# Six of eight f pairs by seven products, and four of their low parts on VectorE

## The chip, the cores and the metric

The kernel runs on one core of one Trainium2 chip. The metric is device time in microseconds, the median of several executions. Before the change it is 857.11 us over three runs (855.28 to 857.62).

## The reference

Strided and local attention over 8 batches, 8 heads, 576 positions and head size 64 gives `x` of 4608 tokens by 512. A feed-forward layer follows, and all of it is float32:

```python
h = x @ w_in            # 4608 x 512 by 512 x 2048
g = h * np.cos(h)
return (g @ w_out)      # 4608 x 2048 by 2048 x 512
```

## The kernel before, in words

The first stage (some 480 us) does the attention and `h = x @ w_in`, and writes `h` to DRAM as `h_all`. The second stage computes `g = h cos(h)` and `g @ w_out`. The change touches the second stage and, by one more set of weight sums, the end of the first.

The second stage walks over 18 blocks of 256 tokens (`s`); in each block it walks over 8 pairs of f tiles (`f`, 256 rows of `w_out` each). Every float32 factor is split into a high part (`g_hi`, a cast on ScalarE, line 183) and a low part (`g_lo`, the value minus its high part, line 184, on VectorE or GpSimd), and each product takes three matmuls: high by high, high by low, low by high (line 709).

A pair is multiplied in one of two ways. A plain pair takes 12 matmuls of 512 columns. A pair "by seven products" uses a Strassen-Winograd scheme on 2 by 2 blocks: 21 matmuls of 256 columns. For that, GpSimd first makes four sums of blocks of `g` (lines 674, 675 and 678, a chain of three instructions), and the split covers 896 columns instead of 512. `SEVEN` lists these pairs; in blocks 2 to 16 all of it holds, in block 1 the first three of it, and blocks 0 and 17 are plain throughout.

`gate(s, f)` (line 642) prepares a pair in four steps: load `h_in`; round on ScalarE and reduce the angle on VectorE (lines 654, 655); the sine on ScalarE, the product `g` on VectorE (line 664 for a plain pair, 673 for one by seven) and the sums on GpSimd; the split. `LEADS` says how many pairs ahead of the multiplication each step is issued (first tuple plain, second by seven). GpSimd's instructions for the gates are held in the order of issue by `by_gpsimd`. `BY_VECTOR` lists plain pairs whose low part is on VectorE. There the product lies in PSUM (tile `wave`); otherwise it lies in SBUF (`r`, or `g` for a pair by seven). Pools: `gp` holds 3 pairs of `g_hi`, `g_lo`; `rp` 3 tiles `r`; `sg` 3 tiles `wave`.

Five PSUM tiles (`q0` to `q4`) take the sums of a block in turn: lower and upper half of the output, and two (more, most) for terms of the seven products. At the end of a block VectorE adds them up (lines 747, 749, 752, then 761 twice), and the next block writes into the tiles that this frees: its upper half into the old "more" as soon as line 747 has read it, its "more" into the old "most" after line 752.

The weights' block sums are made and stored to DRAM in the first stage, loaded again (`t_all`) and split in the second; the last of them go through two buffers `t`.

Of the kernel before, what the change touches and what calls it, by code (L numbers as in the profile page):

```python
# [26 lines left out]
P = 128  # L27
# [52 lines left out]

TB = 2 * P
NTB = NTOK // TB
SEVEN = (4, 5, 6, 1, 2)
ROWS = (0, 3, 7)


LEADS = ((6, 4, 3, 2), (7, 4.5, 3.5, 2))
AHEAD = tuple(PER_BATCH - n for n in (20, 17, 13, 10, 7, 3))

BY_VECTOR = (0, 3, 7)  # L90


SUMMED = (14, 28, 36)
# [9 lines left out]
def attention_cos_ffn(ctx, tc, qkl, vl, qkvs, w_in, w_out, eye, eye16, mask_l0, mask_l, mask_s, out):  # L103
    nc = tc.nc
# [18 lines left out]
    w_all = dram.tile([NFC, P, DM], F32, name="w_all")  # L123
    t_all = dram.tile([len(SEVEN), P, 2 * DM], F32, name="t_all")

# [8 lines left out]
    def order(later, first, reason):  # L134
        tc.add_manual_dep(
            later.ins, first.ins.name,
            mybir.DependencyInfo(mybir.DependencyClass.NoSync, mybir.DependencyReason.DATA), reason=reason,
        )
# [12 lines left out]
    def with_product(begun):  # L151
        if turn is not None:
            order(begun, turn, "with this product")

    def weight_tile(f):
        pool, n = (by_rows, len(ROWS)) if f in ROWS else (wp, NF - len(ROWS))
        return pool.tile([P, 2, 2, 2 * P], F32R, name="w", bufs=2 * n)
# [24 lines left out]
    def split(x, hi, lo, cast=nc.scalar.copy, rest=nc.gpsimd):  # L182
        with_product(cast(out=hi, in_=x))  # L183
        return rest.tensor_tensor(out=lo, in0=x, in1=hi.bitcast(F32), op=ALU.subtract)  # L184
# [401 lines left out]
    def output_weights(room, n, rest=nc.gpsimd):  # L586
        both = room()
        t = weight_tile(n // 2).rearrange("p l m n -> p l (m n)")
        nc.sync.dma_start(out=both, in_=w_all[n])
        yield  # L590
        split(both, t[:, 0], t[:, 1], rest=rest)
        wo.append((t[:, 0], t[:, 1]))
        yield

    def whole_tile(cv):
        return cv.tile([P, 512, 2], I32, name="raw", bufs=3).bitcast(F32).rearrange("p n w -> p (n w)")

    def output_sums(cv, n):

        f = SEVEN[n]  # L600
        both = whole_tile(cv).rearrange("p (f n) -> p f n", f=2)
# [12 lines left out]
    def split_sums(room, n):  # L614
# [6 lines left out]
        split(t[:, :3], most[:, 0], most[:, 1])  # L621
        sums[SEVEN[n]] = [(most[:, 0, n], most[:, 1, n]) for n in range(3)]
        yield
# [3 lines left out]
        split(t[:, 3], *last)  # L627
        sums[SEVEN[n]].append(last)
        yield
# [3 lines left out]
    def seven(s, f):  # L633
        return 0 < s < NTB - 1 and f in SEVEN[:len(SUMMED) if s == 1 else len(SEVEN)]

    of_gates = []

    def by_gpsimd(begun):
        if of_gates:
            order(begun, of_gates[-1], "pair by pair")  # L640
        of_gates.append(begun)

    def gate(s, f):

        h = hp.tile([P, 2 * TB], F32, name="h_in")
        nc.sync.dma_start(
            out=h.rearrange("p (f t) -> p f t", f=2),
            in_=h_all[2 * f:2 * f + 2, :, s * TB:(s + 1) * TB].rearrange("f p t -> p f t"),
        )
        yield  # L650
        r = rp.tile([P, 2 * TB], F32, name="r")
        wave = sg.tile([P, 2 * TB], F32, name="wave")
        k = wave.bitcast(I32)
        with_product(nc.scalar.activation(out=k, in_=h, func=AF.Copy, scale=1.0 / (2.0 * math.pi), bias=0.25))  # L654
        nc.vector.scalar_tensor_tensor(out=r, in0=k, scalar=-2.0 * math.pi, in1=h, op0=ALU.mult, op1=ALU.add)  # L655
        yield
        sin = nc.scalar.activation(out=wave, in_=r, func=AF.Sin, bias=quarter)  # L657
        with_product(sin)
        if s == 0 and f == 0:
            order(sin, exps[-1], "one change of tables")  # L660
        pool = nc.gpsimd
        if not seven(s, f):
            low, pool = (wave, nc.vector) if f in BY_VECTOR else (r, nc.gpsimd)
            nc.vector.tensor_tensor(out=low, in0=wave, in1=h, op=ALU.mult)
            yield
            g_hi, g_lo = (gp.tile([P, 7 * P], F32R, name=name) for name in ("g_hi", "g_lo"))
            lo = split(low, g_hi[:, :4 * P], g_lo[:, :4 * P], rest=pool)
            if pool is nc.gpsimd:
                by_gpsimd(lo)
            gates[s, f] = g_hi, g_lo  # L670
            yield
        g = gs.tile([P, 8, P], F32, name="g")
        nc.vector.tensor_tensor(out=g[:, :4].rearrange("p n t -> p (n t)"), in0=wave, in1=h, op=ALU.mult)
        by_gpsimd(pool.tensor_tensor(out=g[:, 4], in0=g[:, 0], in1=g[:, 2], op=ALU.add))
        by_gpsimd(pool.tensor_tensor(  # L675
            out=g[:, 5:7], in0=g[:, 0:5:4], in1=g[:, 1:2].broadcast_to([P, 2, P]), op=ALU.subtract
        ))
        by_gpsimd(pool.tensor_tensor(out=g[:, 7], in0=g[:, 3], in1=g[:, 6], op=ALU.subtract))  # L678
        yield
        g_hi, g_lo = (gp.tile([P, 7 * P], F32R, name=name) for name in ("g_hi", "g_lo"))  # L680
        by_gpsimd(split(g[:, 1:].rearrange("p n t -> p (n t)"), g_hi, g_lo))
        gates[s, f] = g_hi, g_lo
        yield

    tiles = [(s, f) for s in range(NTB) for f in range(NF)]
    work = [gate(*tile) for tile in tiles]

    def ahead(at):
        for i, tile in enumerate(tiles):
            if i - at in LEADS[seven(*tile)]:  # L690
                next(work[i])
# [90 lines left out]
    with ExitStack() as phase:  # L782
# [18 lines left out]
        m, n, o = ((pools[name], name) for name in "mno")  # L801
# [62 lines left out]
        def in_steps(work, *slots):  # L864
            work = iter(work)
            for slot in slots:
                steps.setdefault(slot, []).append(partial(next, work, None))
# [10 lines left out]
        for n in range(NFC - LATE):  # L878
            at = (B - 1) * PER_BATCH + STEP * (n // 2) + 12 + 3 * (n % 2)
            in_steps(output_weights(lambda: whole_tile(cv)[:, :DM], n), at - 6, at)  # L880
        for n, f in enumerate(SEVEN):
            at = 2 * PER_BATCH + 17 * (2 * f + 2)
# [12 lines left out]
        for slot in range(max(*plan, *steps) + 1):  # L895
# [9 lines left out]
            if b == B - 1:  # L905
                if at == 0:
                    attention.close()
                    sg = ctx.enter_context(tc.tile_pool(
                        name="sg", bufs=3, space=bass.MemoryType.PSUM, side="right", reuse_waits="tile"
# [10 lines left out]

    op = ctx.enter_context(tc.tile_pool(name="op", bufs=2, reuse_waits="tile"))
    tp = ctx.enter_context(tc.tile_pool(name="tp", bufs=1, reuse_waits="tile"))
    gs = ctx.enter_context(tc.tile_pool(name="gs", bufs=3, reuse_waits="tile"))
    pools = {"q": ctx.enter_context(
        tc.tile_pool(name="ps_q", bufs=1, space=bass.MemoryType.PSUM, reuse_waits="tile")
    )}
# [2 lines left out]
    for n in range(NFC - LATE, NFC):  # L929
        rest = nc.vector if n % 2 else nc.gpsimd  # L930
# [115 lines left out]
```

## Time and profile before

| | |
|---|---|
| median of three runs | 857.11 us |
| profiled execution | 857.26 us, of which the span is 855.5 us |
| TensorE busy | 845.1 us, 99% of the span |
| VectorE, ScalarE, GpSimd busy | 567.4, 528.4, 539.7 us |
| mean granted TensorE clock | 0.998 of full speed |

The chain of waits is the row of work that ended last, followed back from the end; in the second stage it is all TensorE. The question for such a kernel is how long a block takes on TensorE, and how far the other engines are from being late for it.

### The profile page before, as it was taken

What the parts mean: (1) busy time and instruction counts of PE and PEld (TensorE: products, weight loads), DVE (VectorE), ACT (ScalarE), POOL (GpSimd) and SP (SyncE); (2) the same over time, 40 slices, a digit from 0 to 9 for tenths busy, and PEclk for the clock granted to TensorE, in tenths of its full rate; (3) what the DMA queues carried; (4) which work ended last, traced back from release to release, by engine and by line L of the source; (5) the groups of instructions that cost most, each with busy time, mean ns of one, the idle gap of its engine ahead of it and who ended that gap; (6) DMA issues with size and microseconds to landing.
All of it is one profiled execution on the core that took longest, in us unless ns stands there. A gap on an engine that the chain in (4) does not pass through costs nothing.

```text
span 855.5 us, 23160 instructions
## 1 busy us (share of the span) xinstructions
PE 845.1 (99%) x9147; PEld 785.3 (92%) x9147; DVE 567.4 (66%) x1087; ACT 528.4 (62%) x1031; POOL 539.7 (63%) x543
## 2 busy tenths in 40 slices
PE   9999999999999999999999999999999999999998
PEld 5799999999998999999999889999999999999996
DVE  5888755768658567676333667777777677767671
ACT  3766545545445354454456887777777777777772
POOL 2578984416207134162166478999899989898951
PEclk9999999999999999999999999999999999999999
DMA  9698444566666667665456844444444444444330
GB/s 333 189 297 296 145 163 165 178 214 207 224 222 208 230 222 226 227 213 210 155 195 222 280 135 129 131 124 125 129 131 124 132 128 124 134 126 136 120 127 26
DMA packets 91901, 151.82 MB, mean 177 GB/s; under 512 B 8464, under 2 KB 53008, under 8 KB 91792
## 3 DMA queue, kind: packets, MB, share of 16 engines
q1 hardware_dynamic: 91072, 150.11, 53.8%
q8 instruction: 72, 1.18, 0.6%
q14 instruction: 37, 0.30, 0.1%
q10 hardware_dynamic: 720, 0.23, 0.1%
HBM read 96.30 MB, written 54.00 MB: 176 GB/s over the span
## 4 chain that ended last, share of the span: by engine, by line
PE 90%; POOL 3%; ACT 2%; DVE 2%; DMA 1%; issue 1%; DVEq 0%; ACTq 0%; POOLq 0%
PE q L709 44%; PE m L532 19%; PE n L532 9%; PE o L532 5%; PE m L503 4%; PE acc L335 2%; PE acc L400 2%; PE acc L318 2%; POOL x_lo L184 2%; PE acc L387 1%; PE acc L811 1%; PE acc L370 1%; DMA h_all<-h 1%; DMA w_all<-sums 1%; PE m L370 0%
## 5 line engine op out<-in xcount | busy, mean ns | idle before, releaser
L709 PE MATMUL q<-w,g_hi 128*128 128x512 f32 (+1 forms) x1000 | 199.9, 338 | 0.0
L709 PEld LDWEIGHTS q<-w,g_hi 128*128 128x128 f32 x1000 | 159.7, 188 | 22.1
L184 POOL TENSOR_TENSOR g_lo<-g,g_hi 128x896 fp32r<-128x896 f32 x78 | 165.1, 2132 | 6.3 <-ACT g_hi L183 6.0
L709 PE MATMUL q<-w,g_lo 128*128 128x512 f32 (+1 forms) x500 | 111.4, 337 | 0.0
L532 PE MATMUL m<-x_hi,v 128*128 128x288 f32 x448 | 109.4, 299 | 0.8 <-ACT m L540 0.8
L532 PE MATMUL m<-x_hi,w 128*128 128x288 f32 x448 | 108.5, 298 | 0.4 <-DVE h L550 0.4
L655 DVE SCALAR_TENSOR_TENSOR r<-wave,h_in 128x512 f32<-128x512 int32 x144 | 96.1, 685 | 15.2 <-ACT wave L654 13.8
L657 ACT ACTIVATE wave<-r,quarter 128x512 f32<-128x512 f32 x144 | 98.6, 688 | 5.9 <-DVE r L655 5.9
L183 ACT CAST g_hi<-g 128x896 fp32r<-128x896 f32 x78 | 73.4, 941 | 39.6 <-POOL g L678 27.7
L709 PEld LDWEIGHTS q<-w,g_lo 128*128 128x128 f32 x500 | 82.7, 188 | 10.9
L654 ACT ACTIVATE wave<-h_in 128x512 int32<-128x512 f32 x144 | 83.6, 591 | 7.6 <-DVE g_lo L184 7.4
L709 PE MATMUL q<-v,g_hi 128*128 128x256 f32 x624 | 85.4, 279 | 0.0
L532 PEld LDWEIGHTS m<-x_hi,v 128*128 128x128 f32 x448 | 78.1, 188 | 2.1 <-ACT m L540 1.3
L532 PEld LDWEIGHTS m<-x_hi,w 128*128 128x128 f32 x448 | 78.0, 188 | 1.4 <-DVE h L550 0.7
L709 PEld LDWEIGHTS q<-v,g_hi 128*128 128x128 f32 x624 | 78.3, 188 | 0.0
L288 POOL TENSOR_TENSOR pn_s<-e_sb,z 128x324 f32<-128x324 f32 x28 | 20.9, 748 | 90.2 <-DVE z L286 84.0
L184 DVE TENSOR_TENSOR g_lo<-wave,g_hi 128x512 fp32r<-128x512 f32 x54 | 37.2, 689 | 53.2 <-PE q L709 36.0
L540 ACT COPY m<-m 128x288 f32<-128x288 f32 x112 | 44.5, 397 | 43.7 <-PE m L532 37.0
L288 POOL TENSOR_TENSOR e_sb<-e_sb,z 128x384 f32<-128x384 f32 x24 | 20.3, 844 | 77.6 <-DVE z L286 77.2
L532 PE MATMUL m<-x_lo,v 128*128 128x288 f32 x224 | 66.1, 295 | 0.0
L532 PE MATMUL m<-x_lo,w 128*128 128x288 f32 x224 | 65.9, 294 | 0.0
L675 POOL TENSOR_TENSOR g<-g 128x256 f32<-128x256 f32 x78 | 57.7, 740 | 6.1
(137 smaller groups left out, 2051.8 us busy)
## 6 DMA issues: line engine op xcount, KB each, us to landing
h_all<-h SPq DMA_DIRECT2D x128, 288.0 KB, 2.9
h_in<-h_all SPq DMA_DIRECT2D x144, 256.0 KB, 2.8
qk<-in_qkvs SPq DMA_DIRECT2D x28, 324.0 KB, 4.4
out<-o SPq DMA_DIRECT2D x35, 256.0 KB, 3.0
qk<-in_qkl SPq DMA_DIRECT2D x21, 416.0 KB, 4.4
raw<-in_w_in SPq DMA_DIRECT2D x16, 512.0 KB, 5.3
raw<-in_w_out SPq DMA_DIRECT2D x16, 512.0 KB, 4.8
v<-in_vl SPq DMA_DIRECT2D x24, 224.0 KB, 4.0
```

What stands on the lines that cost most here:

```text
L183: with_product(cast(out=hi, in_=x))
L184: return rest.tensor_tensor(out=lo, in0=x, in1=hi.bitcast(F32), op=ALU.subtract)
L288: nc.gpsimd.tensor_tensor(out=pn, in0=e, in1=z[:, :n].unsqueeze(2).broadcast_to([P, n, w]), op=ALU.mult)
L318: self.scored = self.pe(nc.tensor.matmul(s_ps[quarter_of(c), t * KW:(t + 1) * KW], q_t[half(j), p, QB * t:QB * (t + 1)], k_t[half(j), p, Q ...
L503: in_turn(nc.tensor.matmul(self.banks[i, j], a[:, c * P:(c + 1) * P], y[:, c], start=k == 0 and m == 0, stop=k == 1 and m == len(ops) - 1, ...
L532: in_turn(nc.tensor.matmul(bank, a[:, c * P:(c + 1) * P], y[:, c], start=first and i == 0, stop=i == len(ops) - 1, skip_group_check=True,))
L540: nc.scalar.copy(out=t, in_=self.bank[name[0]])
L654: with_product(nc.scalar.activation(out=k, in_=h, func=AF.Copy, scale=1.0 / (2.0 * math.pi), bias=0.25))
L655: nc.vector.scalar_tensor_tensor(out=r, in0=k, scalar=-2.0 * math.pi, in1=h, op0=ALU.mult, op1=ALU.add)
L657: sin = nc.scalar.activation(out=wave, in_=r, func=AF.Sin, bias=quarter)
L675: by_gpsimd(pool.tensor_tensor(out=g[:, 5:7], in0=g[:, 0:5:4], in1=g[:, 1:2].broadcast_to([P, 2, P]), op=ALU.subtract))
L709: in_turn(nc.tensor.matmul(at, a, w, start=first, stop=True, skip_group_check=True))
```

## The change

Pair 3 joins the pairs by seven products, in blocks 2 to 16. The gates by seven are begun a pair earlier (loads 8 pairs ahead, rounding 5.5, sine and sums 4.5; the split stays at 2), and `gs`, which holds `g`, has a fourth buffer. The low parts are dealt out anew: of pairs 1, 3, 4 and 6 on VectorE, of 0, 2, 5 and 7 on GpSimd, whichever way the pair is multiplied. Before, VectorE had those of the plain pairs 0, 3 and 7. Output weights of pair 3 are no longer kept in the pool `by_rows`, and a sixth set of weight sums is made, stored, loaded and split.

```diff
-SEVEN = (4, 5, 6, 1, 2)
-ROWS = (0, 3, 7)
+SEVEN = (4, 5, 6, 1, 2, 3)
+ROWS = (0, 7)

-LEADS = ((6, 4, 3, 2), (7, 4.5, 3.5, 2))
+LEADS = ((6, 4, 3, 2), (8, 5.5, 4.5, 2))

-BY_VECTOR = (0, 3, 7)
+BY_VECTOR = (1, 3, 4, 6)
...
         pool = nc.gpsimd
+        rest = nc.vector if f in BY_VECTOR else pool
         if not seven(s, f):
-            low, pool = (wave, nc.vector) if f in BY_VECTOR else (r, nc.gpsimd)
+            low = wave if f in BY_VECTOR else r
             nc.vector.tensor_tensor(out=low, in0=wave, in1=h, op=ALU.mult)
             yield
             g_hi, g_lo = (gp.tile([P, 7 * P], F32R, name=name) for name in ("g_hi", "g_lo"))
-            lo = split(low, g_hi[:, :4 * P], g_lo[:, :4 * P], rest=pool)
-            if pool is nc.gpsimd:
+            lo = split(low, g_hi[:, :4 * P], g_lo[:, :4 * P], rest=rest)
+            if rest is pool:
                 by_gpsimd(lo)
...
         g_hi, g_lo = (gp.tile([P, 7 * P], F32R, name=name) for name in ("g_hi", "g_lo"))
-        by_gpsimd(split(g[:, 1:].rearrange("p n t -> p (n t)"), g_hi, g_lo))
+        lo = split(g[:, 1:].rearrange("p n t -> p (n t)"), g_hi, g_lo, rest=rest)
+        if rest is pool:
+            by_gpsimd(lo)
...
-    gs = ctx.enter_context(tc.tile_pool(name="gs", bufs=3, reuse_waits="tile"))
+    gs = ctx.enter_context(tc.tile_pool(name="gs", bufs=4, reuse_waits="tile"))
```

Lines from 662 on move down by one to three: 664 becomes 665; 673, 674, 675, 678 become 674, 675, 676, 679; 747, 749, 752, 761 become 750, 752, 755, 764.

VectorE at the end of a steady block, before the change. `t` and `o` are the adding up of the block that ends, `q` its PSUM tiles, `wave` 10637 belongs to the plain pair 3 of the next block.

```order
L664 TENSOR_TENSOR wave_10637<-wave_10637,h_in_10561 128x512
L747 TENSOR_TENSOR t_10629<-q1_10430,t_10629 128x256
L749 TENSOR_TENSOR t_10629<-q2_10441,t_10629 128x512
L752 TENSOR_TENSOR t_10629<-q2_10441,t_10629 128x256
L673 TENSOR_TENSOR g_10683<-wave_10651,h_in_10563 128x512
L761 TENSOR_TENSOR o_10660<-q3_10400,t_10629 128x512
L761 TENSOR_TENSOR o_10663<-q4_10405,t_10629 128x512
L655 SCALAR_TENSOR_TENSOR r_10688<-wave_10689,h_in_10600 128x512
L184 TENSOR_TENSOR g_lo_10697<-wave_10637,g_hi_10696 128x512
```

The same place after the change; `g_lo` 10767 is the low part of pair 1 of the next block, 10829 that of pair 3.

```order
L674 TENSOR_TENSOR g_10779<-wave_10753,h_in_10654 128x512
L184 TENSOR_TENSOR g_lo_10767<-g_10671,g_hi_10766 128x896
L750 TENSOR_TENSOR t_10763<-q1_10551,t_10763 128x256
L752 TENSOR_TENSOR t_10763<-q2_10562,t_10763 128x512
L674 TENSOR_TENSOR g_10815<-wave_10785,h_in_10693 128x512
L755 TENSOR_TENSOR t_10763<-q2_10562,t_10763 128x256
L655 SCALAR_TENSOR_TENSOR r_10820<-wave_10821,h_in_10730 128x512
L764 TENSOR_TENSOR o_10794<-q3_10519,t_10763 128x512
L764 TENSOR_TENSOR o_10797<-q4_10524,t_10763 128x512
L184 TENSOR_TENSOR g_lo_10829<-g_10747,g_hi_10828 128x896
```

A low part of 896 columns stands ahead of the first addition, and another right behind the last; before, a low part of 512 columns out of PSUM stood one instruction behind the last.

VectorE in the second half of a block, before. `wave` 10775 and 10799 belong to pair 7 and the next pair 0, `g` 10852 to pair 1 of the next block.

```order
L664 TENSOR_TENSOR wave_10775<-wave_10775,h_in_10700 128x512
L655 SCALAR_TENSOR_TENSOR r_10816<-wave_10817,h_in_10741 128x512
L664 TENSOR_TENSOR wave_10799<-wave_10799,h_in_10739 128x512
L184 TENSOR_TENSOR g_lo_10828<-wave_10775,g_hi_10827 128x512
L673 TENSOR_TENSOR g_10852<-wave_10817,h_in_10741 128x512
```

And after; `g_lo` 10645 is the low part of pair 6, `g` 10671 the product of pair 1 of the next block.

```order
L655 SCALAR_TENSOR_TENSOR r_10633<-wave_10634,h_in_10549 128x512
L665 TENSOR_TENSOR r_10613<-wave_10614,h_in_10547 128x512
L655 SCALAR_TENSOR_TENSOR r_10650<-wave_10651,h_in_10584 128x512
L184 TENSOR_TENSOR g_lo_10645<-g_10568,g_hi_10644 128x896
L674 TENSOR_TENSOR g_10671<-wave_10634,h_in_10549 128x512
```

The product that GpSimd's next chain of sums starts from now stands behind a low part that reads `g` and `g_hi`, both in SBUF.

GpSimd in a steady block before: two chains of sums and their two low parts.

```order
L674 TENSOR_TENSOR g_10308<-g_10308 128x128
L675 TENSOR_TENSOR g_10308<-g_10308 128x256
L678 TENSOR_TENSOR g_10308<-g_10308 128x128
L674 TENSOR_TENSOR g_10345<-g_10345 128x128
L675 TENSOR_TENSOR g_10345<-g_10345 128x256
L678 TENSOR_TENSOR g_10345<-g_10345 128x128
L184 TENSOR_TENSOR g_lo_10361<-g_10308,g_hi_10360 128x896
L184 TENSOR_TENSOR g_lo_10395<-g_10345,g_hi_10394 128x896
```

And after: the low part of plain pair 0 (from `r`), the sums of pairs 3 and 4, and the low part of pair 2.

```order
L184 TENSOR_TENSOR g_lo_10442<-r_10365,g_hi_10441 128x512
L675 TENSOR_TENSOR g_10462<-g_10462 128x128
L676 TENSOR_TENSOR g_10462<-g_10462 128x256
L679 TENSOR_TENSOR g_10462<-g_10462 128x128
L675 TENSOR_TENSOR g_10494<-g_10494 128x128
L676 TENSOR_TENSOR g_10494<-g_10494 128x256
L679 TENSOR_TENSOR g_10494<-g_10494 128x128
L184 TENSOR_TENSOR g_lo_10516<-g_10425,g_hi_10515 128x896
```

There are six chains of sums in a block now, and two low parts of 896 columns and two of 512 between them, where there were five and five.

## Rows read from the trace of the kernel before

**Rows 1.** The page's first part: busy time of each engine.

```profile
span 855.5 us, 23160 instructions
...
PE 845.1 (99%) x9147; PEld 785.3 (92%) x9147; DVE 567.4 (66%) x1087; ACT 528.4 (62%) x1031; POOL 539.7 (63%) x543
```

**Rows 2.** Chain of waits from 480 us on: start, length, what.

```profile
480.00 371.92 PE q L709 x2431
```

**Rows 3.** Timeline of TensorE in one block: start, length, instructions, merged.

```profile
645.06 1.98 PE L709 MATMUL q<-w,g_hi 128*128 128x512 f32 x8
...
647.78 0.86 PE L709 MATMUL q<-w,g_hi 128*128 128x256 f32 x6
...
650.23 0.86 PE L709 MATMUL q<-w,g_hi 128*128 128x256 f32 x6
...
652.68 2.00 PE L709 MATMUL q<-w,g_hi 128*128 128x512 f32 x8
...
655.43 0.86 PE L709 MATMUL q<-w,g_hi 128*128 128x256 f32 x6
...
662.78 2.01 PE L709 MATMUL q<-w,g_hi 128*128 128x512 f32 x8
```

**Rows 4.** Busy time by engine in that block: PE, PEld, DVE, ACT, POOL.

```profile
645.06:665.55 20.49, 20.49 (x143) 19.01 (x141) 15.22 (x27) 16.19 (x27) 17.76 (x21) 1.00 0.43 130
```

**Rows 5.** Timeline of GpSimd in the second stage, three places.

```profile
503.22 1.29 POOL L184 TENSOR_TENSOR g_lo<-r,g_hi 128x512 fp32r<-128x512 f32 x1
504.48 0.45 POOL L674 TENSOR_TENSOR g<-g 128x128 f32<-128x128 f32 x1
...
641.48 0.46 POOL L674 TENSOR_TENSOR g<-g 128x128 f32<-128x128 f32 x1 [0.22 <-DVE g L673]
...
642.02 0.74 POOL L675 TENSOR_TENSOR g<-g 128x256 f32<-128x256 f32 x1
...
642.84 0.46 POOL L678 TENSOR_TENSOR g<-g 128x128 f32<-128x128 f32 x1
...
643.26 4.30 POOL L184 TENSOR_TENSOR g_lo<-g,g_hi 128x896 fp32r<-128x896 f32 x2
...
656.05 4.21 POOL L184 TENSOR_TENSOR g_lo<-g,g_hi 128x896 fp32r<-128x896 f32 x2
...
660.21 0.47 POOL L674 TENSOR_TENSOR g<-g 128x128 f32<-128x128 f32 x1
```

**Rows 6.** Timeline of VectorE and GpSimd in the first stage, around line 469.

```profile
145.82 1.42 POOL L184 TENSOR_TENSOR x_lo<-t,x_hi 128x576 fp32r<-128x576 f32 x1 [1.05 <-ACT x_hi L183]
...
151.57 1.43 POOL L184 TENSOR_TENSOR x_lo<-x,x_hi 128x576 fp32r<-128x576 f32 x1
...
151.65 1.96 DVE L469 TENSOR_TENSOR t<-x,t 128x576 f32<-128x576 f32 x1
...
152.96 1.94 POOL L184 TENSOR_TENSOR x_lo<-t,x_hi 128x576 fp32r<-128x576 f32 x1
```

**Rows 7.** Line 469: instructions, shortest, median and longest duration in ns.

```profile
L469 DVE TENSOR_TENSOR t<-x,t x14: 741/1214/1969, 90.2 to 432.2; 128x576 f32<-128x576 f32 x14
```

**Rows 8.** Timeline of ScalarE and VectorE around a block's end.

```profile
641.75 0.95 ACT L183 CAST g_hi<-g 128x896 fp32r<-128x896 f32 x1 [0.24 <-PE q L709]
...
643.22 0.37 ACT L746 COPY t<-q 128x256 f32<-128x256 f32 x1
...
643.92 0.41 DVE L747 TENSOR_TENSOR t<-q,t 128x256 f32<-128x256 f32 x1
...
649.05 0.69 DVE L655 SCALAR_TENSOR_TENSOR r<-wave,h_in 128x512 f32<-128x512 int32 x1
...
649.65 0.69 DVE L673 TENSOR_TENSOR g<-wave,h_in 128x512 f32<-128x512 f32 x1
```

**Rows 9.** Who waited for whom, 520 to 835 us: total, times, longest.

```profile
ACT g_hi L183 <- PE q L709: 33.0, 72, 1.2
DVE g_lo L184 <- PE q L709: 30.5, 24, 3.2
```

## The prediction

> **What bounds the kernel now.** I read the page's busy times first: TensorE is busy for 99% of the span, every other engine for 62 to 66% [rows 1]. That is a mean over two stages, so the chain of waits comes next: from 480 us to the end it is one piece of 371.92 us of TensorE at line 709 [rows 2]. The second stage costs what TensorE's matmuls cost, as long as nobody is late for it.
>
> The timeline of TensorE then gives the price of a pair [rows 3]. A pair by seven products takes 650.23 - 647.78 = 2.45 us and again 652.68 - 650.23 = 2.45 us; plain pair 3 takes 655.43 - 652.68 = 2.75 us. The block from 645.06 takes 20.49 us, and TensorE is busy for all of it [rows 4].
>
> Last I look at who is near to being late. ScalarE and VectorE wait for TensorE, 33.0 and 30.5 us in all [rows 9], so they are ahead of it. GpSimd looks free at 17.76 of 20.49 us [rows 4], but its timeline counts otherwise [rows 5]. A chain of sums takes 643.26 - 641.48 = 1.78 us from its start to the next instruction, since the second and third instruction each start 0.08 us after the one before has ended; a low part of 896 columns takes (660.21 - 656.05)/2 = 2.08 us. Five of each make 19.30 us. GpSimd has 1.19 us to spare in a block, and no more.
>
> **The change part by part.** *Pair 3 by seven products.* TensorE saves 2.75 - 2.45 = 0.30 us a block, so a block could take 20.19 us. Blocks 2 to 16 have it, 15 in all: 4.5 us. That is the whole of the gain, and it is had only if the others deliver a block in 20.19 us.
>
> *GpSimd's own work.* A sixth chain of sums comes, three low parts of 896 columns go, two of 512 come, each 504.48 - 503.22 = 1.26 us [rows 5]. The new sum is 6 x 1.78 + 2 x 2.08 + 2 x 1.26 = 10.68 + 4.16 + 2.52 = 17.36 us. Taken alone it would leave 2.83 us of 20.19.
>
> *Four low parts of 896 columns on VectorE.* Before, VectorE's low parts read `wave` from PSUM and `g_hi` from SBUF. The new ones read both `g` and `g_hi` from SBUF. In the second stage's steady blocks there is no such instruction; the nearest is line 469 in the first stage, 576 columns with both inputs in SBUF. Its shortest takes 0.741 us, its median 1.214, its longest 1.969 [rows 7], and the timeline shows why [rows 6]. The one at 151.65 started 0.08 us behind a GpSimd instruction that ran until 153.00 and itself ended at 153.61, 0.61 us after that; the next GpSimd instruction, begun at 152.96, took 1.94 us where its like takes 1.42. Each waited for the other. VectorE had its turn between two GpSimd instructions, and GpSimd lost 0.52 us to 0.61 us of VectorE's.
>
> For 896 columns I scale that: VectorE's turn is 0.61 x 896/576 = 0.95 us, and GpSimd loses 0.52 + (0.95 - 0.61) = 0.86 us. Where the turn falls inside a chain of sums, GpSimd would have stood still anyway: there the next instruction starts 0.08 us late, elsewhere 0.04 us before the last has ended [rows 5], so the loss is 0.12 us less, 0.74 us. Four turns cost GpSimd between 0 (if all fell where it waits anyway) and 4 x 0.86 = 3.44 us. All four in chains give 17.36 + 2.96 = 20.32 us a block, none in a chain 20.80. I take two and two: 17.36 + 3.20 = 20.56 us. I take none as free, because a GpSimd that needs over 20 us of a block has no idle time for them to fall into.
>
> So the bound passes from TensorE's 20.49 us to GpSimd's 20.56 us, and 15 blocks cost 15 x 0.07 = 1.05 us more. Against this stands, once, the lateness that can build up before TensorE notices. The tightest place is the end of a block: line 747 ended at 643.92 + 0.41 = 644.33 [rows 8], and the tile that it reads is written again after the first four matmuls of the next block, 645.06 + 4 x 2.72/12 = 645.97 [rows 3]. That is 1.64 us, in which the first blocks after block 1 run at 20.19. The sum against the profiled 857.26 us is 857.26 + 1.05 - 1.64 = 856.67.
>
> On this the Trainium skill has a rule (SBUF — State Buffer, "Who interferes with whom"): a VectorE instruction with two SBUF inputs and a GpSimd instruction that reads SBUF exclude each other, and the one that starts second is blocked until the other has ended. The trace agrees that they exclude each other. It shows less for the price: of an instruction that alone takes 0.74 us, 0.52 us is lost to GpSimd. By the rule to its letter the price is a rival, below.
>
> *VectorE.* It is busy for 15.22 us of a block [rows 4]. Three low parts of 512 go, at 649.65 - 649.05 = 0.60 us each back to back [rows 8]; four of 896 come, alone 0.741 + 0.34 = 1.08 us, back to back 0.09 less (0.69 - 0.60): 15.22 - 1.80 + 3.96 = 17.38 us. To each comes a wait for GpSimd between 0 and 2.08 us; 0.7 us on the mean would fill 20.19. The wait that matters is the one of pair 1, which stands ahead of the additions. Its cast ends at about 641.75 + 0.95 = 642.70, and line 747 waited for ScalarE until 643.59 anyway, so the low part alone hides there and 1.64 us of wait are covered; without that cover TensorE stops.
>
> *ScalarE.* One cast of 896 for one of 512 adds less than the 0.95 us of the whole cast to 16.19 us [rows 4, 8]: at most 17.14, no bound.
>
> *The rest.* The earlier steps and the fourth `g` move no work, they give room. The third load of `t` stands in SyncE's queue until GpSimd has split the first, with `h_in` loads behind it; those are now issued 8 pairs ahead, and if one were late after all it would cost less than a pair, 2.75 us, once. I take 0. The sixth set of weight sums in the first stage runs beside TensorE; 0. Blocks 0, 1 and 17 keep TensorE's 2.75 us for their plain pairs, and only deal out low parts otherwise; 0.
>
> The profiled execution stands 0.15 us above the median of the three runs; so 856.5.
>
> **The rivals.** *TensorE stays the bound.* If GpSimd loses 0.70 us or less a turn, 17.36 + 2.80 = 20.16 fits under 20.19, and the time is 857.26 - 4.5 - 0.15 = 852.6. For it: my 0.86 is scaled from 576 columns, the bound from below is 0, and a turn may fall where GpSimd waits for a cast or a product and lose nothing. Against it: the 0.52 us at 576 columns [rows 6], and that a GpSimd so full seldom waits.
>
> *GpSimd waits for VectorE as well.* The product of pair 1 of the next block stands on VectorE right behind the low part of pair 6. If that low part comes while GpSimd works on pair 5's, it waits for its end; GpSimd, done, then has its next chain of sums to begin, and stands idle for VectorE's turn and the product, 0.95 + 0.69 = 1.64 us, where I counted 0.80. The block is 20.56 + 0.84 = 21.40 us, the time 857.26 + 15 x 0.91 - 1.64 - 0.15 = 869.1; with every other block so, 862.8. It decides from a block of 20.77 us on (over 2.6 us in all after the 1.64). For it: the order of the two engines. Against it: once GpSimd is late enough, VectorE's low part of pair 6 comes before pair 5's and the product is early, so it should cure itself.
>
> *The whole instruction is lost.* With 1.08 us a turn, GpSimd needs 17.36 + 4.32 = 21.68 us, and the time is 857.26 + 15 x 1.19 - 1.64 - 0.15 = 873.3. That is what the Trainium skill's rule comes to (SBUF — State Buffer). Rows 6 speak against it.
>
> **How the numbers follow.** My forecast, no change, has 0.42; TensorE as the bound 0.30; GpSimd's wait 0.25; the whole instruction 0.03. About 0.3% (2.6 us) can be told from no change here. Faster is the first rival, 0.30; slower the other two, 0.28; the forecast reaches from 20.36 us to 20.77 us a block. The range goes from just under the first rival, 852.3, to somewhat beyond the second with every other block, 865; beyond it I leave 0.15. The likeliest case alone runs from 854 to 860.
>
> **What would show it.** After the change, line 709's pair 3 at 2.45 us, and stalls of TensorE, which are none now, in some blocks of the later part. A block of 20.19 throughout means the first rival. The low parts on VectorE should show from 1.08 us up to 3, and GpSimd's sums beside them 0.7 to 0.9 us longer than now. If those stay as short as now, the two don't exclude each other here and I am wrong at the root. Idle of GpSimd before line 675 for VectorE's product, over 1 us a block, means the second rival.

## The result, and the profile after

The changed kernel takes 870.19 us (868.28 to 870.92, five runs) against 857.11 us (855.28 to 858.43, five runs): a ratio of 1.0143, 95% interval 1.0129 to 1.0156. The forecast of 856.5 us was wrong, and so was its range, which ended at 865. The time is close to that of the second rival, 869.1 us.

The page of the profiled execution (870.77 us), first the busy time of each engine and then the shares of the chain of waits:

```profile
span 869.0 us, 23409 instructions
PE 843.8 (97%) x9282; PEld 786.7 (91%) x9282; DVE 638.5 (73%) x1105; ACT 530.6 (61%) x1033; POOL 544.7 (63%) x575
...
PE 58%; POOL 23%; ACT 6%; DVE 5%; issue 4%; DMA 3%; SPq 0%; POOLq 0%; DVEq 0%; ACTq 0%
```

TensorE was busy for 99% of the span in [rows 1] and for 97% now. GpSimd, which had no part in the second stage's chain [rows 2], now has 23% of the whole one, though it is busy for only 5.0 us more. VectorE has 71.1 us more of busy time. Some 40 us of that is waiting that the trace counts as busy: its 62 low parts of 896 columns take 108.1 us, and at 1.09 us each, the shortest, they would take 67.6.

Line 749, ScalarE's copy, comes once at the end of each block. Its row gives the first and the last of 16, in the kernel before and then in this one:

```profile
L746 ACT COPY t<-q x16: 363/370/374, 520.3 to 827.3; 128x256 f32<-128x256 f32 x16
```

```profile
L749 ACT COPY t<-q x16: 354/358/367, 522.4 to 841.2; 128x256 f32<-128x256 f32 x16
```

The 15 blocks between them took 307.0 us and now take 318.8. Of the 13.5 us between the two spans, 11.8 are there. 2.1 us lie ahead of the first copy, and 0.4 us were won behind the last. The 2.1 us can't be put down to the change: in the profiled runs below the first copy starts between 519.9 and 523.3 us, and in two runs of one and the same kernel at 520.1 and 521.1.

Block by block the distance is 20.21 us, then 21.23, then 21.45 within 0.03, and 19.96 for the last. The windows of the first of these blocks and of a later one (sum of the stretch, then busy time of TensorE, its weight loads, VectorE, ScalarE and GpSimd; they answer to [rows 4]):

```profile
522.36:542.57 20.21, 20.21 (x152) 19.24 (x151) 17.49 (x26) 15.96 (x27) 17.72 (x21) 1.00 0.44 130
...
628.12:649.59 21.47, 20.50 (x152) 19.13 (x151) 19.41 (x26) 15.84 (x26) 18.90 (x23) 1.00 0.41 123
```

The first block is what TensorE alone would need, 20.19 as foretold. In the later one TensorE stands still for 0.97 us, at 2.4 GHz (granted clock 1.00) in both. GpSimd's timeline of that later block shows why it is 21.47 us long; it answers to [rows 5] (start, duration, engine, line; in brackets the idle time before and who ended it):

```profile
628.89 1.30 POOL L675 TENSOR_TENSOR g<-g 128x128 f32<-128x128 f32 x1
...
631.51 0.46 POOL L675 TENSOR_TENSOR g<-g 128x128 f32<-128x128 f32 x1
...
633.29 2.14 POOL L184 TENSOR_TENSOR g_lo<-g,g_hi 128x896 fp32r<-128x896 f32 x1
635.39 1.31 POOL L675 TENSOR_TENSOR g<-g 128x128 f32<-128x128 f32 x1
636.78 0.73 POOL L676 TENSOR_TENSOR g<-g 128x256 f32<-128x256 f32 x1
637.59 1.19 POOL L679 TENSOR_TENSOR g<-g 128x128 f32<-128x128 f32 x1
638.74 0.46 POOL L675 TENSOR_TENSOR g<-g 128x128 f32<-128x128 f32 x1
...
640.52 2.13 POOL L184 TENSOR_TENSOR g_lo<-g,g_hi 128x896 fp32r<-128x896 f32 x1
644.28 0.46 POOL L675 TENSOR_TENSOR g<-g 128x128 f32<-128x128 f32 x1 [1.63 <-DVE g L674]
```

A sum of 128 columns takes 0.46 us undisturbed, at 631.51 and 638.74. At 628.89 it took 1.30 (0.84 more), at 635.39 1.31 (0.85 more), and at 637.59, inside a chain, 1.19 (0.73 more). At 642.65, behind the low part begun at 640.52, GpSimd stood idle for 1.63 us until VectorE's product was there. The own work of 17.36 us and these four make 17.36 + 0.84 + 0.85 + 0.73 + 1.63 = 21.41 us, against 21.45 measured: the block is as long as GpSimd's round.

VectorE in the same block:

```profile
628.33 1.55 DVE L184 TENSOR_TENSOR g_lo<-g,g_hi 128x896 fp32r<-128x896 f32 x1
629.80 0.41 DVE L750 TENSOR_TENSOR t<-q,t 128x256 f32<-128x256 f32 x1
...
633.58 2.79 DVE L184 TENSOR_TENSOR g_lo<-g,g_hi 128x896 fp32r<-128x896 f32 x1
...
636.90 1.56 DVE L184 TENSOR_TENSOR g_lo<-g,g_hi 128x896 fp32r<-128x896 f32 x1
...
642.29 1.31 DVE L184 TENSOR_TENSOR g_lo<-g,g_hi 128x896 fp32r<-128x896 f32 x1
643.52 0.68 DVE L674 TENSOR_TENSOR g<-wave,h_in 128x512 f32<-128x512 f32 x1
```

The four low parts are those of pairs 1, 3, 4 and 6. The one at 633.58 began 0.29 us behind GpSimd's of 633.29 and lasted until GpSimd's was over (635.43) and 0.94 us more. The last, of pair 6, stands ahead of the product of pair 1 of the next block, and that product is what GpSimd waited for. Why it comes so late is on ScalarE:

```profile
638.81 0.94 ACT L183 CAST g_hi<-g 128x896 fp32r<-128x896 f32 x1 [3.23 <-POOL g L679]
639.66 0.59 ACT L654 ACTIVATE wave<-h_in 128x512 int32<-128x512 f32 x1
640.19 0.67 ACT L657 ACTIVATE wave<-r,quarter 128x512 f32<-128x512 f32 x1
640.81 0.58 ACT L654 ACTIVATE wave<-h_in 128x512 int32<-128x512 f32 x1
641.33 0.93 ACT L183 CAST g_hi<-g 128x896 fp32r<-128x896 f32 x1
642.17 0.68 ACT L657 ACTIVATE wave<-r,quarter 128x512 f32<-128x512 f32 x1
```

ScalarE waited 3.23 us with the cast of pair 5 for GpSimd's sums of pair 5, which end at 638.78. Behind that cast stand, in ScalarE's order, two roundings, a sine, the cast of pair 6 (641.33) and the sine of the next pair 1 (642.17). So VectorE's low part of pair 6 can't start before 642.26, and the product, and GpSimd's next sums, come behind it. It is a loop: a late GpSimd makes ScalarE late, ScalarE makes VectorE late, and VectorE makes GpSimd wait.

The waits of 520 to 845 us (waiter, line, for whom; total, times, longest) answer to [rows 9]:

```profile
ACT g_hi L183 <- POOL g L679: 60.4, 29, 3.2
POOL g L675 <- DVE g L674: 22.8, 14, 1.6
ACT g_hi L183 <- PE q L712: 17.3, 19, 1.2
...
PE q L712 <- DVE t L750: 11.7, 12, 1.0
```

ScalarE waited for TensorE before; now it waits for GpSimd. Fourteen times GpSimd waits for a product. TensorE's own stalls, twelve of about 1.0 us, are at the end of a block, for line 750:

```profile
628.23 1.07 PE L712 MATMUL q<-w,g_hi 128*128 128x512 f32 x4
630.27 1.19 PE L712 MATMUL q<-w,g_hi 128*128 128x512 f32 x4 [0.97 <-DVE t L750]
...
637.12 0.86 PE L712 MATMUL q<-w,g_hi 128*128 128x256 f32 x6
...
639.58 0.86 PE L712 MATMUL q<-w,g_hi 128*128 128x256 f32 x6
```

From 637.12 to 639.58 is pair 3, by seven products: 2.46 us, as foretold.

### The profile page after: what moved, and what is told of

It reads as the page before. It is cut to its first block, busy times and chain, and to the rows that moved or that the text cites. A ratio compares the mean times of both kernels' runs of the same rounds, so it can differ in the third digit from the quotient of the medians.

```text
span 869.0 us, 23409 instructions
## 1 busy us (share of the span) xinstructions
PE 843.8 (97%) x9282; PEld 786.7 (91%) x9282; DVE 638.5 (73%) x1105; ACT 530.6 (61%) x1033; POOL 544.7 (63%) x575
## 4 chain that ended last, share of the span: by engine, by line
PE 58%; POOL 23%; ACT 6%; DVE 5%; issue 4%; DMA 3%; SPq 0%; POOLq 0%; DVEq 0%; ACTq 0%
PE m L532 19%; PE q L712 14%; PE n L532 9%; POOL g_lo L184 6%; POOL g L675 5%; POOL g L676 5%; PE o L532 5%; PE m L503 4%; POOL g L679 4%; DMA h_all<-h 2%; PE acc L335 2%; ACT g_hi L183 2%; PE acc L400 2%; PE acc L318 2%; DVE g L674 1%
## 5 line engine op out<-in xcount | busy, mean ns | idle before, releaser
L712 PE MATMUL q<-w,g_hi 128*128 128x256 f32 (+1 forms) x970 | 186.5, 328 | 11.7 <-DVE t L750 11.7
L712 PEld LDWEIGHTS q<-w,g_hi 128*128 128x128 f32 x970 | 147.8, 188 | 33.4 <-DVE t L750 17.2
L183 ACT CAST g_hi<-g 128x896 fp32r<-128x896 f32 x93 | 87.4, 939 | 78.7 <-POOL g L679 59.9
L184 DVE TENSOR_TENSOR g_lo<-g,g_hi 128x896 fp32r<-128x896 f32 x62 | 108.1, 1743 | 3.9 <-ACT g_hi L183 2.3
L712 PE MATMUL q<-w,g_lo 128*128 128x256 f32 (+1 forms) x485 | 103.1, 326 | 0.0
L712 PE MATMUL q<-v,g_hi 128*128 128x256 f32 x744 | 101.9, 279 | 0.0
L712 PEld LDWEIGHTS q<-v,g_hi 128*128 128x128 f32 x744 | 93.5, 188 | 0.0
L675 POOL TENSOR_TENSOR g<-g 128x128 f32<-128x128 f32 x93 | 69.3, 745 | 22.8 <-DVE g L674 22.8
L184 POOL TENSOR_TENSOR g_lo<-r,g_hi 128x512 fp32r<-128x512 f32 x41 | 53.6, 1308 | 24.9 <-ACT g_hi L183 11.0
L674 DVE TENSOR_TENSOR g<-wave,h_in 128x512 f32<-128x512 f32 x93 | 63.4, 682 | 6.2 <-ACT wave L657 6.2
```

Source lines behind the costliest of these rows:

```text
L712: in_turn(nc.tensor.matmul(at, a, w, start=first, stop=True, skip_group_check=True))
```

## The experiments

Each kernel was timed beside the kernel before on the same chip; the ratio is to that (857.11 to 859.76 us, so times of different rows compare by their ratios). "Own" is GpSimd's own work in a block from the durations of [rows 5], "turns" what its instructions beside VectorE's took longer than undisturbed, "waits" its idle time for a product. E5 was timed twice.

| kernel | time, us | ratio, 95% | GpSimd: own + turns + waits | a block, us |
|---|---|---|---|---|
| changed | 870.19 | 1.0129 to 1.0156 | 17.36 + 2.43 + 1.63 = 21.42 | 21.45 |
| E1 | 881.95 | 1.0252 to 1.0316 | 19.30 + 2.43 + 0.31 = 22.04 | 22.1 |
| E2 | 859.14 | 0.9994 to 1.0018 | 19.30 | 20.49 |
| E3 | 859.48 | 0.9983 to 1.0019 | under the block | 20.54 |
| E4 | 858.08 | 0.9976 to 1.0003 | 18.18 + 2.37 + 0 = 20.55 | 20.54 |
| E5 | 854.64, 854.46 | 0.9928 to 0.9967, 0.9944 to 0.9973 | under the block | 20.17 |
| E6 | 875.43 | 1.0165 to 1.0216 | 16.92 + 2.43 + 2.15 = 21.50 | 21.57 |
| E7 | 873.58 | 1.0169 to 1.0205 | 17.36 + 3.17 + 0.96 = 21.49 | 21.68 |
| E8 | 861.25 | 1.0028 to 1.0055 | 17.36 + 3.30 + 0 = 20.66 | 20.67 |
| E9 (one round) | 899.95 | 1.0436 to 1.0519 | 6 x 3.86 = 23.16 | 23.16 |
| E10 | 865.24 | 1.0064 to 1.0102 | 16.92 + 2.45 + 1.45 = 20.82 | 20.83 |

**E1 and E2: is it the two inputs in SBUF, or VectorE's time?** Both are the kernel before with passes on VectorE added whose result nobody reads: E1 three a block of 896 columns with both inputs in SBUF, E2 five a block of 512 columns with one input in PSUM.

```diff
+        if s > 1 and f in (1, 4, 6):                                        # E1
+            nc.vector.tensor_tensor(
+                out=idle, in0=g[:, 1:].rearrange("p n t -> p (n t)"), in1=g_hi.bitcast(F32), op=ALU.subtract
+            )
```

```diff
+        if s > 1:                                                           # E2
+            nc.vector.tensor_tensor(out=idle, in0=wave, in1=h, op=ALU.mult)
```

> The kernel before, with three more VectorE instructions in each block from block 2 to 16 (pairs 1, 4, 6): the subtraction of 896 columns with both inputs in SBUF, into a tile that nobody reads. If VectorE's and GpSimd's SBUF inputs exclude each other at 0.85 us a turn: GpSimd's block is 19.30 + 3 x 0.85 = 21.85 us against 20.49 of TensorE, so 15 x 1.36 less 1.6 of lateness, some 19 us slower, about 876 us. If it is VectorE's own time that made the changed kernel slow: 15.22 + 3 x 0.99 = 18.2 us of 20.49, no change, 857 us, and the same as the kernel with passes out of PSUM.

> The kernel before, with five more VectorE instructions in each block from block 2 to 16: the product of 512 columns once more, one input in PSUM, into a tile that nobody reads; 5 x 0.60 = 3.0 us of VectorE a block, as much as three low parts of 896 columns take alone. If exclusion of SBUF inputs is the cause: no change, 857 us, GpSimd's instructions as long as before. If VectorE's own time is the cause: as slow as the kernel with passes out of SBUF.

E1 is 2.8% slower, by 23 us where 19 were expected; E2 is not slower at all. GpSimd's instructions by line and shape, 560 to 800 us (total and mean ns behind the bar), in E1 and then in E2, and E2's own passes:

```profile
L184 POOL TENSOR_TENSOR g_lo<-g,g_hi 128x896 fp32r<-128x896 f32 x54 | 126.8, 2366 | 0.0
L678 POOL TENSOR_TENSOR g<-g 128x128 f32<-128x128 f32 x55 | 39.4, 716 | 4.3
```

```profile
L184 POOL TENSOR_TENSOR g_lo<-g,g_hi 128x896 fp32r<-128x896 f32 x59 | 125.1, 2134 | 0.6
...
L675 DVE TENSOR_TENSOR idle<-wave,h_in 128x512 f32<-128x512 f32 x59 | 40.0, 679 | 0.0
```

In E1 a low part is 0.23 us and the third sum 0.25 us longer on the mean, for five of each 2.4 us a block: three turns of about 0.8 us. GpSimd also stands idle for 0.31 us a block, which the expectation didn't have. In E2 five passes of 0.68 us leave GpSimd's low part at 2134 ns; in the kernel before it takes 2132 on the mean. What costs GpSimd is not VectorE's time but the second SBUF input. The Trainium skill (SBUF — State Buffer, "Who interferes with whom") says as much: a VectorE instruction with at most one SBUF input, outside its 2-port modes, doesn't contend with GpSimd; one with two contends with a GpSimd instruction that reads SBUF. Both runs agree.

**E4: the low part of pair 6 taken away from VectorE.** It goes to GpSimd, and that of pair 0, out of PSUM, to VectorE.

```diff
-BY_VECTOR = (1, 3, 4, 6)
+BY_VECTOR = (0, 1, 3, 4)
```

> The changed kernel with pair 6's low part back on GpSimd and plain pair 0's on VectorE out of PSUM. If the block is GpSimd's sum with three turns, and its wait for the product of pair 1 goes because no low part of 896 columns stands ahead of that product any more: 10.68 + 3 x 2.08 + 1.26 + 3 x 0.85 = 20.73 us, so 857.3 + 15 x 0.24 - 1.6, about 859 us. If the wait stays (1.63 us in 21.45): 22.3 us a block, about 883 us. If VectorE's in-order queue as such is the cause: VectorE has less to do by 0.4 us and its waits, some 864 to 868 us.

GpSimd's own work grows by 0.82 us, and the block gets 0.91 us shorter. GpSimd's sums, 560 to 800 us:

```profile
L679 POOL TENSOR_TENSOR g<-g 128x128 f32<-128x128 f32 x71 | 49.7, 700 | 5.6
L675 POOL TENSOR_TENSOR g<-g 128x128 f32<-128x128 f32 x71 | 44.1, 622 | 0.0
```

Line 675 had 22.8 us of idle time for products in the changed kernel; here it has none. The turns are there still: (0.70 - 0.46) + (0.62 - 0.46) = 0.40 us on the mean, for six of each 2.4 us. Without the wait a block is own work and turns, 20.55.

E4 doesn't show that the product came in time, though. VectorE and GpSimd in one of its blocks:

```profile
638.80 0.69 DVE L674 TENSOR_TENSOR g<-wave,h_in 128x512 f32<-128x512 f32 x1 [0.69 <-ACT wave L657]
```

```profile
636.45 4.23 POOL L184 TENSOR_TENSOR g_lo<-g,g_hi 128x896 fp32r<-128x896 f32 x2
```

The two low parts are those of pairs 5 and 6. The product of pair 1 waited for its sine on ScalarE and ended at 639.49, some 0.9 us after the low part of pair 5 (about 638.6), with no low part ahead of it on VectorE. GpSimd wasn't idle because it had the low part of pair 6 to do in that time.

**E8: the gates by seven begun one pair sooner still.** The product of pair 1 then stands ahead of the low part of pair 6 on VectorE; who does which low part stays.

```diff
-LEADS = ((6, 4, 3, 2), (8, 5.5, 4.5, 2))
+LEADS = ((6, 4, 3, 2), (9, 6.5, 5.5, 2))
...
-    gs = ctx.enter_context(tc.tile_pool(name="gs", bufs=4, reuse_waits="tile"))
+    gs = ctx.enter_context(tc.tile_pool(name="gs", bufs=5, reuse_waits="tile"))
```

> The changed kernel with the gates by seven begun one more pair sooner (9, 6.5, 5.5, 2; a fifth buffer of g), which puts the product of pair 1 ahead of the low part of pair 6 on VectorE. If GpSimd's 1.63 us of waiting for that product is what takes the block from 20.56 to 21.45 us: the wait goes, the four turns stay, 20.4 to 20.7 us, 855 to 859 us. If the turns alone make the block (the wait only moves elsewhere): 21.4 us as before, 869 to 871 us.

GpSimd's sums again:

```profile
L675 POOL TENSOR_TENSOR g<-g 128x128 f32<-128x128 f32 x70 | 62.2, 889 | 0.0
L676 POOL TENSOR_TENSOR g<-g 128x256 f32<-128x256 f32 x70 | 60.7, 867 | 5.5
```

Again no idle time for products, and now all four turns are paid: (0.89 - 0.46) + (0.87 - 0.74) = 0.56 us, for six 3.3 us, where the prediction took 3.20. At 861.25 us the kernel is somewhat above the 855 to 859 expected, also when that is counted from 858.83 us for the kernel before, but the block is as expected. The block is 20.67 us; the prediction's 20.56 is nearly what this kernel does, not the changed one. So two ways of taking the wait away, one by other work for GpSimd and one by an earlier product, take away what the prediction missed.

**E3: the new dealing with pair 3 plain, as before.**

```diff
-SEVEN = (4, 5, 6, 1, 2, 3)
+SEVEN = (4, 5, 6, 1, 2)
```

> The changed kernel with pair 3 plain again (five pairs by seven), all else as changed: low parts of pairs 1, 4, 6 (896 columns) and of plain pair 3 (from PSUM) on VectorE, of 2, 5 (896) and 0, 7 (512) on GpSimd. By the theory (GpSimd's sum with turns): 5 x 1.78 + 2 x 2.08 + 2 x 1.26 + 3 x 0.8 = 18.0 us, under TensorE's 20.49, so no change from before, 857 us, though VectorE and GpSimd still exclude each other. If the new dealing-out harms by itself, with the queue's order at a block's end: over 860 us.

No change can be seen against the kernel before. The earlier start and the fourth buffer are in this kernel too. The dealing of five pairs does no harm; the sixth pair, with its chain of sums and its turn, is needed as well for GpSimd to be late.

**E7: the gates by seven begun when they were before.**

```diff
-LEADS = ((6, 4, 3, 2), (8, 5.5, 4.5, 2))
+LEADS = ((6, 4, 3, 2), (7, 4.5, 3.5, 2))
```

> The changed kernel with the gates by seven begun as late as before the change (7, 4.5, 3.5, 2), all else as changed. If the wait of GpSimd for VectorE's product belongs to the loop (sums, cast, low part of pair 6, product, sums): the loop stays, and with a pair less of room the block is 21.45 us or longer, 870 us or more. If it was the sooner start, with its fuller buffers, that harmed: 860 us or less.

It is slower than the changed kernel (intervals that don't meet), so beginning sooner helped a little. The wait for the product is shorter, and the turns are dearer:

```profile
656.36 1.47 POOL L676 TENSOR_TENSOR g<-g 128x256 f32<-128x256 f32 x1
...
662.01 0.47 POOL L675 TENSOR_TENSOR g<-g 128x128 f32<-128x128 f32 x1 [0.96 <-DVE g L674]
```

The 0.19 us that the table's account leaves open are a second, shorter wait. VectorE's product begun at 657.75 ends at 658.43, and GpSimd's sum that needs it begins at 658.50, 0.14 us behind the end of the one before, where a sum that needn't wait begins 0.04 us ahead of that end.

**E9: all low parts by seven on GpSimd**, those of pairs 0 and 7 on VectorE out of PSUM.

```diff
-BY_VECTOR = (1, 3, 4, 6)
+BY_VECTOR = (0, 7)
```

> The changed kernel with all six low parts of 896 columns on GpSimd, and 0 and 7 on VectorE out of PSUM: no instruction of VectorE with two SBUF inputs in a steady block. GpSimd alone then needs 6 x (1.78 + 2.08) = 23.16 us a block by the rows of before: 857.3 + 15 x 2.67 - 1.6, about 896 us. If GpSimd is not what a block waits for: 853 to 870 us.

Without a single turn GpSimd needs 6 x (1.78 + 2.08) = 23.16 us by [rows 5], and the block takes 23.16. Handing low parts to VectorE is needed with six pairs; the price of a turn, 0.85, is well under the 2.08 that it takes off GpSimd.

**E5 and E6: three turns instead of four.** Low parts of pairs 0 and 7 on VectorE out of PSUM, and three of 896 columns: pairs 2, 3, 4 in E5, pairs 3, 4, 6 in E6. GpSimd's own work is the same.

```diff
-BY_VECTOR = (1, 3, 4, 6)
+BY_VECTOR = (0, 7, 2, 3, 4)          # E5
+BY_VECTOR = (0, 7, 3, 4, 6)          # E6
```

> The changed kernel with VectorE taking the low parts of 2, 3, 4 (896 columns out of SBUF) and of plain 0 and 7 out of PSUM, GpSimd those of 1, 5, 6. By the theory: GpSimd 6 x 1.78 + 3 x 2.08 + 3 x 0.8 = 19.3 us, VectorE some 17.6 us and three waits, both under TensorE's 20.19: the gain of pair 3 comes through, 15 x 0.30 = 4.5 us, some 853 us at a before of 857. If six pairs by seven can't be fed at all, whoever has the low parts: 20.5 us a block or more, 857 us or slower.

> As the kernel with 2, 3, 4 on VectorE, but with 3, 4, 6 (and 0, 7 out of PSUM); GpSimd has 1, 2, 5. Pair 6's low part is on VectorE again, now with the product of pair 1 ahead of it. By the theory GpSimd's sum is the same 19.3 us: some 853 us at a before of 857. If a low part of pair 6 on VectorE harms by its place whatever stands ahead of it: 857 us or slower, and slower than the kernel with 2, 3, 4.

E5 is faster than the kernel before. The window of some two of its blocks shows TensorE busy throughout:

```profile
600.00:641.00 41.00, 41.00 (x308) 39.08 (x307) 36.19 (x54) 32.52 (x53) 37.42 (x43) 1.00 0.42 130
```

Its GpSimd's waits for products, 560 to 800 us, are short, 0.5 us at most:

```profile
POOL g L675 <- DVE g L674: 9.6, 23, 0.5
```

E6 missed by far: 875.43 us, slower than the changed kernel, with the same own work as E5. Its GpSimd waits for the product twice a block:

```profile
653.14 0.47 POOL L675 TENSOR_TENSOR g<-g 128x128 f32<-128x128 f32 x1 [1.67 <-DVE g L674]
...
671.20 0.47 POOL L675 TENSOR_TENSOR g<-g 128x128 f32<-128x128 f32 x1 [0.45 <-DVE g L674]
```

So the number of turns alone doesn't decide: GpSimd's waits come on top. Before the longer wait, three angle reductions stand on VectorE ahead of the product, and the sine that it needs stands on ScalarE behind three roundings and a cast:

```profile
650.07 1.88 DVE L655 SCALAR_TENSOR_TENSOR r<-wave,h_in 128x512 f32<-128x512 int32 x3
652.37 0.69 DVE L674 TENSOR_TENSOR g<-wave,h_in 128x512 f32<-128x512 f32 x1 [0.42 <-ACT wave L657]
```

Further back on the same chain stands the low part of pair 6, the third on VectorE in this block, and ScalarE waits for the reduction behind it (VectorE's two rows, then ScalarE's):

```profile
645.77 1.74 DVE L184 TENSOR_TENSOR g_lo<-g,g_hi 128x896 fp32r<-128x896 f32 x1
647.43 0.68 DVE L655 SCALAR_TENSOR_TENSOR r<-wave,h_in 128x512 f32<-128x512 int32 x1
```

```profile
648.14 0.69 ACT L657 ACTIVATE wave<-r,quarter 128x512 f32<-128x512 f32 x1 [1.40 <-DVE r L655]
```

So the rival in E6's expectation, that a low part of pair 6 on VectorE harms by its place, isn't excluded but borne out by the time, and by this chain. In E4 and E5, where GpSimd has that low part, GpSimd waits 0.5 us at most at a time for a product. This is read from the traces; in E6 neither the low part nor the reductions were taken away by themselves.

**E10: E6 with E8's earlier start.** `BY_VECTOR` as in E6, `LEADS` and `gs` as in E8.

> The kernel with 3, 4, 6 (and 0, 7 out of PSUM) on VectorE, which took 21.57 us a block though GpSimd's instructions and turns sum to 19.4, with the gates by seven begun one more pair sooner (9, 6.5, 5.5, 2; a fifth buffer of g). If GpSimd's waits for VectorE's products (some 2.1 us a block there) make the difference: they go, TensorE is the bound, 20.2 us a block, 4 us faster than before. If the place of pair 6's low part harms by itself: near 21.5 us a block, 16 us slower than before.

It missed by half: 20.83 us a block. One wait for a product is left, 1.39 us:

```profile
667.67 0.47 POOL L675 TENSOR_TENSOR g<-g 128x128 f32<-128x128 f32 x1 [1.39 <-DVE g L674]
```

What holds that product back was not separated.

**E5 again, in more rounds**, since it is the version that beats both kernels:

> The kernel with VectorE taking the low parts of 2, 3, 4 out of SBUF and of 0 and 7 out of PSUM once more, for a closer interval: 20.17 us a block as in its first run, 0.5% faster than before. If its gain was chance: within 0.3% of before.

854.46 against 857.58 us, 0.27 to 0.56% less, and 20.17 us a block again. TensorE is busy for 99% of its span, as before the change.

## Why the prediction was wrong

**Right: the gain on TensorE.** Pair 3 costs 2.46 us, and where nobody is late a block takes 20.21 us, in the changed kernel's first one, and 20.17 throughout E5.

**Right: what GpSimd needs, and the price of a turn.** 0.86 and 0.74 us were worked out from 576 columns; 0.84 to 0.85 and 0.73 were measured. The rival by which the whole 1.08 us is lost falls with it, and so does the one of 0.70 us or less: TensorE didn't stay the bound. The low parts on VectorE, foretold as 1.08 us up to 3 (shortest, median and longest ns):

```profile
L184 DVE TENSOR_TENSOR g_lo<-g,g_hi x60: 1093/1554/2804, 522.5 to 834.8; 128x896 fp32r<-128x896 f32 x60
```

**Wrong: "I take two and two".** The forecast gave the fourth turn, pair 6's, 0.80 us like the others and left GpSimd without idle time. Here that low part begins 0.36 us before GpSimd's low part of pair 5 ends, and what GpSimd then lacks is the product behind it: 1.63 us of idle time. That is the second rival, which priced it at 0.95 + 0.69 = 1.64 us and the block at 21.40; 21.45 was measured. The forecast's reason, that a GpSimd which needs over 20 us of a block has no idle time, fails here: this one needs 19.79 us (17.36 + 2.43) and is idle for 1.63 more.

**Wrong: "so it should cure itself".** This was why the rival had a chance of only 0.25. I reasoned from two engines: with GpSimd late, VectorE's low part of pair 6 would come before GpSimd's of pair 5. The third engine was left out. ScalarE's cast of pair 6 stands behind its cast of pair 5, and that one waits for GpSimd's sums; the later GpSimd is, the later is VectorE's low part of pair 6. The sine for the product stands there as well: it ends at 642.85, so the product could have been some 0.67 us earlier at most if only the low part had stood elsewhere in VectorE's order, and the sine alone would have left GpSimd waiting for some 0.96 us. E4 bears that out, with its product 0.9 us behind pair 5's low part. So the second rival's sum is met nearly to the digit, but its cause, the low part ahead of the product, explains only some 0.67 of the 1.63 us by itself. Shown is that the loss goes when GpSimd gets the low part of pair 6, and with it work for that time (E4), and when the product is moved ahead with its whole gate, the sine too (E8). How it divides between the low part and the sine is argued from the traces; no run moved one without the other.

**Right in place, without weight: TensorE's stall.** It is where the prediction looked, at the upper half of the output behind line 750, but it is a consequence: by GpSimd's account the block is 21.4 us with or without it. GpSimd's wait has its full length already in the first of these blocks, in which TensorE never stood still:

```profile
537.04 0.46 POOL L675 TENSOR_TENSOR g<-g 128x128 f32<-128x128 f32 x1 [1.63 <-DVE g L674]
```

**Right: the lateness before TensorE notices.** 1.64 us was foretold. Against 21.45 us the first block is 1.24 us shorter and the second 0.22, 1.46 us in all. Not counted was the way out: the last block is 1.49 us shorter, since the plain block 17 behind it asks no sums of GpSimd.

**Nothing, as taken:** ScalarE's busy time (15.84 us a block), the sixth set of sums, and blocks 0 and 17.

## What to carry to other kernels

That the sum of an engine's work fits into the period doesn't show that the engine keeps up, if it works in strict order: follow one round through all engines, from the late engine's output to the input that it waits for next, and ask of each queue on the way what stands ahead. Before "it cures itself" is believed, the loop has to be closed over every engine in it. Work handed from GpSimd to VectorE with both inputs in SBUF still costs GpSimd some 40% of what it saves (0.85 of 2.08 us), so hand over first what reads PSUM, and put the rest where nothing that GpSimd waits for stands behind it, on VectorE or by way of ScalarE.

## What the runs showed of the hardware beyond that

What two engines lose to each other stands nowhere as idle time: it lengthens an instruction on each side (a 128-column sum from 0.46 to 1.30 us, a low part from 1.09 to 2.80), so that GpSimd's busy time in a block, 18.90 of 21.47 us, holds 2.4 us of waiting. And the blocks of E1 don't settle at one length but repeat in threes, 21.56, 22.27 and 22.49 us; why was not looked into.
